# y of the later units: the state product as row tiles behind q kᵀ, a compact state, and a new written-out order

## The chip, the cores and the metric

The kernel runs on one core of a Trainium2 chip. The metric is the device time of one execution in microseconds. TensorE is PE in the profile (PEld its weight loads), VectorE is DVE, ScalarE is ACT, GpSimd is POOL, SyncE is SP.

## What is computed

A recurrent attention with a decaying state for 4 batches and 8 heads of width 48 over 768 positions, and behind it a two-layer network with a squared relu:

```python
for t in range(S):
    cur = np.einsum('bhd,bhe->bhde', u[None] * kt, vt)
    y[:, :, t] = np.einsum('bhd,bhde->bhe', rt, state + cur)
    state = w[None, :, :, None] * state + np.einsum('bhd,bhe->bhde', kt, vt)
...
h = x @ w_in
r = np.maximum(h, 0.0)
g = r * r
return (g @ w_out)
```

x is y of all heads side by side, 3072 rows of 384; w_in is 384 x 2048 and w_out 2048 x 384.

## The kernel before

**Units.** The sequence is cut into 6 chunks of 128 positions; a unit is one chunk of one batch, so there are 24, and unit i is chunk i // 4 of batch i % 4. Heads are handled in four pairs p; within a pair, head o = 0 lies on partitions 0 to 63 and head o = 1 on 64 to 127 (48 rows used, 16 zero).

**The order.** A string, SCHEDULE, lists every step as a word, `name:arguments@banks`. The words are run one after the other, each engine takes its own instructions in that order, and nothing reorders them. The numbers behind `@` are the PSUM banks (of 8) that the step's results take. `3*fill@4` is three times the step fill.

**The steps of a unit i.** `load:i:kt|rt|vt:queue` fetches k, r or v (192 KB) on the SP or POOL queue. `scale:i:0` multiplies r by powers of w and `scale:i:1` multiplies k by inverse powers (L287, DVE); the two tables of powers, wpos and wneg, are made once by `power:0` and `power:1` (L240, ACT) from the product of `spread_log` (L236). The scaled r and k are turned: for units 0 to 5 by `turn:i:x` on PE (L310) and `evict_rk:i:x` on ACT (L314), for later ones by `turn_dma:i` (L301, a transposing DMA of the SP queue). `rk` (L319, DVE) multiplies both for the diagonal term. `at:i` (L327) is q kᵀ: 8 matmuls that use 64 rows each, alternating between the two row halves, into two banks; `ats:i` does units i and i+1. `mask:i:o` (L339, DVE) takes out the upper triangle. `sums:i` (L347, L352) makes the diagonal sums and the unit's part of the state; it needs `uwb`, which POOL makes in `u_columns` (L251, L254) from `cols`, which DVE copies in `copy_columns` (L248). POOL also makes the decay over a whole chunk (`end_columns`, L257 and L259) and issues the four pieces of w_in (`win:q:0`, L273) and of w_out (`wout:q:0`, L278).

**y.** `y_mm:i` is 8 matmuls of the masked product with v (L390, 48 columns) and, from chunk 1 on, 4 of the turned r with the state (L396, 128 rows, 96 columns), whose bf16 copy `stb` holds the two heads of a pair as a block diagonal; `state_cast` (L381) writes it in two copies of 64 partitions. All twelve go into one bank. `diag_v` (L361) and `evict_y` (L405) finish y on DVE. `state_add` (L369, L371) and `state_decay` (L375) keep the state on DVE. y is turned by `x_turn` and `evict_x` (L420, L424) for units 0 to 5, and by `x_dma` (L414, SP queue) for later ones.

**The network.** `mm1:i:m:s` (L434) makes part of h for m units at once (m = 1 for units 0 to 7, m = 2 from 8 on); s counts the parts, 4 for m = 1 and 8 for m = 2, and for m = 1 part s needs piece s of w_in. `relu` (L442, ACT) and `square:...:a` (L451 on ACT where a is 1, L453 on DVE where it is 0) follow. `mm2:i:q` (L460) sums a quarter of the second product; `evict_o` (L467) and `store` (L494) bring it out. Unit 23 ends with `mm2_half` (L475), `evict_half` and `store_half` in two pieces.

`fill` (L232) is a matmul on constants whose result is not used: it fills waiting time of PE.

Of the kernel before, what the change touches and what calls it, by code (L numbers as in the profile page):

```python
# [9 lines left out]
BF16 = mybir.dt.bfloat16  # L10
# [12 lines left out]
fill@4 mask:1:1 turn:0:1@0 turn:2:0@1 scale:2:1 evict_rk:0:1 fill@4 fill@6 y_mm:1@2 diag_v:1 fill@6 win:3:0
evict_rk:2:0 2*fill@6 fill@0 rk:0 turn:2:1@3 fill@0 evict_y:1 load:3:vt:POOL evict_rk:2:1 at:0@4,5 2*fill@1 mask:0:0
fill@1 fill@2 cast_v:0 wout:0:0 at:2@6,0 load:6:rt:SP mask:0:1 cast_v:2 fill@3 fill@4 load:4:rt:POOL x_turn:1@1 fill@4
rk:2 sums:0@2 evict_x:1 fill@5 y_mm:0@3 diag_v:0 mm1:1:1:0@4 mask:2:0 wout:1:0 sums:2@5 evict_y:0 2*fill@1 2*fill@6
mask:2:1 x_turn:0@1 load:4:kt:POOL mm1:1:1:1@6 evict_x:0 diag_v:2 fill@0 scale:3:1 y_mm:2@3 relu:1:1:1 2*fill@1
mm1:0:1:0@0 evict_y:2 state_add:1 x_turn:2@1 turn:3:1@6 evict_x:2 mm1:0:1:1@3 evict_rk:3:1 mm1:2:1:0@7 scale:3:0
square:1:1:1:0 mm1:1:1:2@1 wout:2:0 relu:2:1:0 load:6:kt:SP state_add:2 relu:0:1:0 load:4:vt:POOL turn:3:0@6
mm1:0:1:2@7 evict_rk:3:0 mm1:2:1:2@0 relu:0:1:1 rk:3 wout:3:0 square:0:1:0:1 at:3@5,6 relu:1:1:0 load:5:vt:POOL  # L30
mm1:2:1:1@3 mask:3:0 relu:0:1:2 mm1:1:1:3@4 state_add:0 cast_v:3 square:2:1:0:1 mm1:2:1:3@5 square:0:1:1:0
square:1:1:0:1 sums:3@7 mask:3:1 mm1:0:1:3@2 relu:1:1:3 diag_v:3 relu:2:1:1 mm2:2:0@6 scale:4:0 relu:0:1:3 y_mm:3@4
mm2:0:0@3 relu:2:1:3 evict_y:3 relu:1:1:2 turn:4:0@2 x_turn:3@5 square:2:1:1:1 mm2:1:0@4 scale:4:1 evict_x:3
square:2:1:3:0 mm2:0:1 evict_rk:4:0 square:0:1:3:0 square:0:1:2:1 mm2:2:1 state_cast:0 square:1:1:3:0 turn:4:1@1
mm2:1:1 scale:5:1 evict_rk:4:1 mm1:3:1:2@5 square:1:1:2:0 relu:2:1:2 state_add:3 cast_v:4 mm1:3:1:1@2 load:9:kt:SP
mm2:0:2 scale:5:0 relu:3:1:1 load:7:kt:SP turn:5:1@1 state_cast:1 at:4@0,7 mm2:1:2 evict_rk:5:1 mask:4:1 load:8:kt:SP
square:2:1:2:1 turn:5:0@2 mask:4:0 mm1:3:1:0@1 evict_rk:5:0 load:7:rt:SP rk:4 y_mm:4@7 scale:6:0 relu:3:1:0 mm2:2:2
scale:6:1 relu:3:1:2 rk:5 at:5@0,2 cast_v:5 turn_dma:6 sums:4@1 state_cast:3 mm2:0:3 diag_v:4 square:3:1:0:1
mm1:3:1:3@5 mask:5:1 load:8:rt:SP square:3:1:1:1 evict_y:4 load:6:vt:SP mm2:1:3 relu:3:1:3 mask:5:0 sums:5@2
square:3:1:2:1 x_turn:4@7 mm2:2:3 load:9:rt:SP diag_v:5 evict_x:4 scale:7:1 evict_o:0 y_mm:5@5 scale:7:0 mm1:4:1:1@0  # L40
load:7:vt:SP state_add:4 mm1:4:1:0@7 evict_y:5 turn_dma:7 mm2:3:0@3 relu:4:1:0 scale:8:1 evict_o:1 at:6@1,5
square:4:1:0:0 evict_o:2 x_turn:5@7 load:10:kt:SP mm2:3:1 mask:6:0 evict_x:5 mm1:4:1:2@4 load:9:vt:SP scale:9:1 rk:6
mm2:3:2 relu:4:1:2 square:3:1:3:0 mm1:5:1:0@6 cast_v:6 scale:8:0 state_cast:2 sums:6@7 mask:6:1 turn_dma:8 mm2:3:3
square:4:1:2:1 diag_v:6 y_mm:6@1 relu:5:1:0 mm2:4:0@4 relu:4:1:1 evict_y:6 mm1:5:1:1@5 state_add:5 square:4:1:1:1
x_dma:6 rk:7 at:7@6,1 relu:5:1:1 scale:9:0 mm2:4:1 cast_v:7 mask:7:1 turn_dma:9 mm1:5:1:2@0 square:5:1:0:0 sums:7@2
mm1:5:1:3@5 mask:7:0 load:11:rt:SP state_add:6 mm1:4:1:3@1 load:10:rt:SP relu:5:1:3 y_mm:7@6 diag_v:7 load:8:vt:SP
relu:4:1:3 mm2:4:2 state_add:7 square:4:1:3:1 mm1:6:1:0@7 evict_y:7 mm2:4:3 x_dma:7 relu:6:1:0 relu:5:1:2
ats:8@5,1,2,6 square:6:1:0:0 square:5:1:1:1 load:11:vt:SP mm2:5:0@7 mask:8:0 square:5:1:3:1 load:11:kt:SP mm2:5:1
state_decay:5 evict_o:3 mask:8:1 load:12:kt:SP state_cast:5 mm2:6:0@0 state_decay:7 store:3:POOL mask:9:1 mm1:6:1:1@5
state_cast:7 store:1:POOL rk:8 mm1:6:1:3@3 cast_v:9 store:2:POOL rk:9 square:5:1:2:1 scale:10:1 store:0:POOL  # L50
mm1:6:1:2@1 scale:10:0 relu:6:1:1 sums:9@6 mask:9:0 relu:6:1:3 turn_dma:10 mm2:5:2 relu:6:1:2 diag_v:9 y_mm:9@5
cast_v:8 state_decay:4 mm1:7:1:0@3 evict_y:9 square:6:1:1:1 load:12:rt:SP sums:8@2 scale:11:0 state_cast:4 x_dma:9
mm2:6:1 diag_v:8 relu:7:1:0 y_mm:8@1 scale:11:1 mm1:7:1:1@5 state_add:8 turn_dma:11 mm1:7:1:3@3 evict_y:8 relu:7:1:1
square:7:1:0:0 mm1:7:1:2@2 relu:7:1:3 x_dma:8 state_add:9 mm2:5:3 square:6:1:2:1 cast_v:11 square:7:1:1:0 mm2:7:0@1
load:10:vt:SP relu:7:1:2 rk:10 load:13:rt:SP mm2:7:1 state_decay:9 square:7:1:2:0 load:13:kt:SP state_cast:9 mm2:6:2
square:6:1:3:0 square:7:1:3:1 mm2:7:2 load:13:vt:SP rk:11 evict_o:4 mm2:6:3 scale:12:0 evict_o:5 load:14:kt:SP
scale:12:1 ats:10@5,3,6,2 mm1:8:2:0@4 mask:10:1 turn_dma:12 mm1:8:2:4@7 mask:11:1 relu:8:2:0 mask:11:0 mm1:8:2:2@3
cast_v:10 load:14:rt:SP mask:10:0 sums:11@2 mm1:8:2:3@4 diag_v:11 mm1:8:2:1@6 scale:13:0 relu:8:2:3 state_decay:6
sums:10@5 relu:8:2:4 scale:13:1 y_mm:11@4 state_cast:6 mm2:7:3 turn_dma:13 evict_y:11 relu:8:2:2 mm1:8:2:7@7
square:8:2:0:0 relu:8:2:1 diag_v:10 y_mm:10@4 x_dma:11 square:8:2:3:1 mm1:8:2:6@3 square:8:2:1:0 square:8:2:4:1  # L60
mm1:8:2:5@6 evict_y:10 relu:8:2:6 load:12:vt:SP square:8:2:2:0 mm2:9:0@4 x_dma:10 relu:8:2:5 state_add:11 mm2:9:1
square:8:2:5:1 state_add:10 mm2:8:0@3 cast_v:13 load:15:kt:SP evict_o:6 state_decay:10 load:15:rt:SP mm2:8:1
relu:8:2:7 scale:14:1 load:16:kt:SP store:6:POOL evict_o:7 mm2:8:2 state_decay:8 rk:13 state_cast:8 store:4:POOL
square:8:2:7:0 ats:12@6,2,5,0 store:5:POOL scale:14:0 mm2:9:2 mask:13:1 turn_dma:14 sums:13@7 mm1:10:2:0@1
# [52 lines left out]
def kernel(  # L117
# [427 lines left out]
```

## Time and profile before

| | us |
|---|---|
| three runs: median (lowest to highest) | 174.15 (173.06 to 174.81) |
| the profiled execution | 172.5 |
| its span, first to last instruction | 170.4 |
| PE busy in the span | 163.4 |
| DVE busy | 137.0 |
| ACT busy | 120.9 |

The granted TensorE clock is 1.000 over the span. In the views below, times are microseconds from the span's start, and a row of the chain or the timeline gives a start, a length, the engine and line, and how many instructions were merged. A matmul's row includes its way through the array, so the pace of a group is read from the start of one group to the start of the next.

### The profile page before, as it was taken

What the parts mean: (1) busy time and instruction counts of PE and PEld (TensorE: products, weight loads), DVE (VectorE), ACT (ScalarE), POOL (GpSimd) and SP (SyncE); (2) the same over time, 40 slices, a digit from 0 to 9 for tenths busy, and PEclk for the clock granted to TensorE, in tenths of its full rate; (3) what the DMA queues carried; (4) which work ended last, traced back from release to release, by engine and by line L of the source; (5) the groups of instructions that cost most, each with busy time, mean ns of one, the idle gap of its engine ahead of it and who ended that gap; (6) DMA issues with size and microseconds to landing.
All of it is one profiled execution on the core that took longest, in us unless ns stands there. A gap on an engine that the chain in (4) does not pass through costs nothing.

```text
span 170.4 us, 4781 instructions
## 1 busy us (share of the span) xinstructions
PE 163.4 (96%) x1917; PEld 129.9 (76%) x1917; DVE 137.0 (80%) x297; ACT 120.9 (71%) x253; POOL 30.5 (18%) x62
## 2 busy tenths in 40 slices
PE   3899999999999999999999999999999999999993
PEld 2467998778778786795796895896898776999662
DVE  5359969969998999799988979988999898664800
ACT  3355489997685988579499499599359985295830
POOL 7989540000000500001100001203000030030010
PEclk9999999999999999999999999999999999999999
DMA  6999999989999999998999994998989994150014
GB/s 115 188 220 211 221 248 244 227 155 129 187 159 187 209 237 133 192 207 131 250 203 116 200 217 81 251 192 176 252 100 212 197 159 139 27 162 0 4 63 167
DMA packets 94784, 28.83 MB, mean 169 GB/s; under 512 B 90665, under 2 KB 92714, under 8 KB 94762
## 3 DMA queue, kind: packets, MB, share of 16 engines
q1 hardware_dynamic: 90512, 19.08, 73.9%
q0 software_dynamic: 4224, 9.44, 21.4%
q8 instruction: 15, 0.25, 0.6%
q14 instruction: 7, 0.06, 0.2%
q10 hardware_dynamic: 26, 0.00, 0.0%
HBM read 20.45 MB, written 4.72 MB: 148 GB/s over the span
## 4 chain that ended last, share of the span: by engine, by line
PE 84%; DVE 6%; DMA 5%; issue 1%; ACT 1%; ACTq 1%; DVEq 0%
PE bank L434 35%; PE bank L460 31%; PE bank L327 4%; DMA xT<-yb 3%; PE bank L390 3%; DMA rkT<-rkw 2%; PE bank L352 2%; PE bank L232 2%; PE bank L396 2%; PE bank L310 2%; PE bank L475 2%; DVE am L339 1%; DVE rkw L287 1%; PE bank L347 1%; DVE g L453 1%
## 5 line engine op out<-in xcount | busy, mean ns | idle before, releaser
L442 ACT ACTIVATE gr<-bank 128x512 f32<-128x512 f32 x96 | 53.1, 603 | 27.3 <-PE bank L434 25.9
L434 PE MATMUL bank<-xT,w_in_q 128*128 128x128 bf16 (+1 forms) x768 | 70.8, 246 | 0.6 <-DMA xT<-yb 0.4
L460 PE MATMUL bank<-w_out_q,g 128*128 128x384 bf16 x368 | 68.1, 327 | 0.1
L434 PEld LDWEIGHTS <-w_in_q 128*128 128x128 bf16 x768 | 64.2, 113 | 3.4 <-DMA xT<-yb 0.5
L460 PEld LDWEIGHTS <-g 128*128 128x128 bf16 x368 | 33.7, 98 | 19.2 <-DVE g L453 0.6
L453 DVE TENSOR_TENSOR g<-gr 128x512 bf16<-128x512 f32 x49 | 32.4, 686 | 6.9 <-ACT gr L442 6.8
L494 POOL DMA_DIRECT2D out_dram<-osb x21 | 11.3, 543 | 129.4 <-ACT osb L467 118.7
L339 DVE TENSOR_TENSOR am<-bank,smask 128x512 bf16<-128x512 f32 x48 | 31.4, 685 | 2.9 <-PE bank L327 2.8
L451 ACT ACTIVATE g<-gr 128x512 bf16<-128x512 f32 x47 | 29.1, 638 | 0.6
L287 DVE TENSOR_TENSOR rkw<-ldk,wneg 128x384 bf16<-128x384 f32 x24 | 13.2, 553 | 4.8 <-ACT wneg L240 3.6
L381 ACT CAST stb<-st 64x192 bf16<-64x192 f32 x40 | 13.9, 348 | 2.6 <-DVE st L375 2.3
L361 DVE TENSOR_TENSOR dv<-vb,bank 128x384 f32<-128x384 bf16 x24 | 13.0, 550 | 2.4 <-PE bank L352 1.5
L405 DVE TENSOR_TENSOR yb<-bank,dv 128x384 bf16<-128x384 f32 x24 | 13.3, 555 | 1.3 <-PE bank L396 0.3
L287 DVE TENSOR_TENSOR rkw<-ldr,wpos 128x384 bf16<-128x384 f32 x24 | 13.1, 553 | 1.0 <-DMA ldr<-in_r_dram 0.8
L319 DVE TENSOR_TENSOR rk<-rkT 128x512 bf16<-128x512 bf16 x24 | 10.0, 420 | 3.8 <-ACT rkT L314 2.0
L467 ACT COPY osb<-bank 128x384 f32<-128x384 f32 x23 | 10.5, 483 | 2.7 <-PE bank L460 2.7
L291 ACT CAST vb<-ldv 128x384 bf16<-128x384 f32 x24 | 12.1, 512 | 0.4 <-DMA ldv<-in_v_dram 0.3
L371 DVE TENSOR_TENSOR st<-bank,st 64x192 f32<-64x192 f32 x32 | 11.2, 351 | 1.2 <-PE bank L352 0.9
L232 PE MATMUL bank<-warm 128*128 128x256 bf16 x39 | 9.2, 334 | 2.0 <-DVE warm L183 1.5
L314 ACT COPY rkT<-bank 128x512 bf16<-128x512 bf16 x12 | 6.9, 595 | 3.7 <-PE bank L310 3.6
L390 PEld LDWEIGHTS <-am 128*128 128x128 bf16 x192 | 7.9, 96 | 2.0 <-issue 0.7
L327 PEld LDWEIGHTS <-rkT 64*128 64x128 bf16 x192 | 5.5, 96 | 4.2 <-issue 3.9
(58 smaller groups left out, 112.2 us busy)
## 6 DMA issues: line engine op xcount, KB each, us to landing
ldk<-in_k_dram SPq DMA_DIRECT2D x22, 192.0 KB, 4.6
out_dram<-osb POOLq DMA_DIRECT2D x21, 192.0 KB, 3.3
ldr<-in_r_dram SPq DMA_DIRECT2D x20, 192.0 KB, 3.7
ldv<-in_v_dram SPq DMA_DIRECT2D x19, 192.0 KB, 4.3
w_in_q<-in_moe_w_in_dram POOLq DMA_DIRECT2D x4, 384.0 KB, 8.9
w_out_q<-in_moe_w_out_dram POOLq DMA_DIRECT2D x4, 384.0 KB, 10.7
ldv<-in_v_dram POOLq DMA_DIRECT2D x5, 192.0 KB, 9.0
ldr<-in_r_dram POOLq DMA_DIRECT2D x4, 192.0 KB, 8.2
```

The lines of the kernel that those rows point to most:

```text
L232: nc.tensor.matmul(out=banks[given.pop(0)][:, :n], lhsT=warm[:, :128], rhs=warm[:, :n], start=True, stop=True)
L287: nc.vector.tensor_tensor(t["rkw"][:, x, :, :, :D], pair(src), pair(wx), ALU.mult)
L339: nc.vector.tensor_tensor(am, t["at"][o], smask.unsqueeze(1).to_broadcast([C, HP, C]), ALU.mult)
L361: nc.vector.tensor_tensor(t["dv"], t["vb"], t["d"].unsqueeze(2).to_broadcast([C, H, D]), ALU.mult)
L381: nc.scalar.copy(stb[b][sl, :, o * D : (o + 1) * D], st32[b][sl])
L390: nc.tensor.matmul(out=y[:, 2 * p + o, :], lhsT=t[f"am{o}"][:, p, :], rhs=t["vb"][:, 2 * p + o, :], start=(o == 0 and p == 0), stop=c == 0 ...
L405: nc.vector.tensor_tensor(t["yb"], t["y"], t["dv"].rearrange("p h d -> p (h d)"), ALU.add)
L434: nc.tensor.matmul(out=t["h", s][:, a], lhsT=turned, rhs=chunks[c]["xT"][:, n, b : b + m, :], start=(n == 0), stop=(n == NK - 1),)
L442: nc.scalar.activation(t["gr", s], t["h", s], AF.Relu)
L451: nc.scalar.activation(g, x, AF.Square)
L453: nc.vector.tensor_tensor(g, x, x, ALU.mult)
L460: nc.tensor.matmul(out=t["o"], lhsT=chunks[units[i][0]]["g"][:, f, units[i][1], :], rhs=w_out_q[f // 4][:, f % 4, :], start=(f == 0), stop ...
```

## The change

From unit 8 on, `ats:i` issues 16 more matmuls behind the 16 of q kᵀ: the turned r times the state, for each head by itself, 64 rows and 48 columns each, alternating between the row halves. The state's bf16 copy for them, `stc`, is 128 x 192 with no block diagonal, and `state_cast` writes it in one copy (for the states that units 8 and later read; units 4 to 7 go on with `stb` and `y_mm`). A new step `ys:i` adds the masked product with v for both units. The y of a pair takes two banks, one for each row half, both units side by side in each, from `ats` until it is evicted; `evict_y` has two instructions of 128 x 4 x 48 in place of one of 128 x 384.

SCHEDULE is written anew from its first line to its last. It has the same loads, stores, casts, turns and matmul steps apart from `y_mm` and `ys`, 38 fills instead of 39, and 8 squares more on ACT and 8 fewer on DVE. Its first lines and the code of the change (line numbers of what follows shift with it):

```diff
-load:1:kt:SP load:1:rt:POOL fill@7 load:0:rt:SP 2*fill@7 load:1:vt:POOL fill@7 load:0:kt:SP 3*fill@7 load:2:kt:SP
...
+load:1:kt:SP load:1:rt:POOL fill@6 load:0:rt:SP 2*fill@6 load:1:vt:POOL load:0:kt:SP load:2:kt:SP constants
...
+    Y_FROM = 8
...
+    stc = [const.tile([128, HP, D], BF16, name=f"stc_{b}") for b in range(B)]
...
+    def halves(i):
+        return [bank("y", i - i % 2, o).rearrange("p (u x) -> p u x", u=2)[:, i % 2, : dm // 2].rearrange("p (a d) -> p a d", a=HP) for o in range(2)]
+
     def ats(i):
         at(i)
         at(i + 1)
+        for j in (i, i + 1):
+            y = halves(j)
+            for p in range(HP):
+                for o in range(2):
+                    sl = slice(o * 64, o * 64 + 64)
+                    nc.tensor.matmul(
+                        out=y[o][:, p, :], lhsT=tiles[j]["rkT"][sl, 0, p, :], rhs=stc[units[j][1]][sl, p, :],
+                        start=(j == i and p == 0), stop=False, skip_group_check=True,
+                    )
...
     def state_cast(i):
         b = units[i][1]
-        for o in range(2):
+        if i >= Y_FROM - B:
+            nc.scalar.copy(stc[b], st32[b])
+        for o in range(2 if i < Y_FROM - B else 0):
             sl = slice(o * 64, o * 64 + 64)
             nc.scalar.copy(stb[b][sl, :, o * D : (o + 1) * D], st32[b][sl])
+
+    def ys(i):
+        for j in (i, i + 1):
+            t = tiles[j]
+            y = halves(j)
+            for p in range(HP):
+                for o in range(2):
+                    nc.tensor.matmul(
+                        out=y[o][:, p, :], lhsT=t[f"am{o}"][:, p, :], rhs=t["vb"][:, 2 * p + o, :],
+                        start=False, stop=j > i and p == HP - 1, skip_group_check=True,
+                    )
...
     def evict_y(i):
         t = tiles[i]
         t["yb"] = buffer("yb", [C, dm], BF16)
+        if i >= Y_FROM:
+            out_y = t["yb"].rearrange("c (a o d) -> c o a d", o=2, d=D)
+            dv = t["dv"].rearrange("c (a o) d -> c o a d", o=2)
+            for o, y in enumerate(halves(i)):
+                nc.vector.tensor_tensor(out_y[:, o], y, dv[:, o], ALU.add)
+            return
         nc.vector.tensor_tensor(t["yb"], t["y"], t["dv"].rearrange("p h d -> p (h d)"), ALU.add)
```

The order as built, at the places that the prediction speaks of. A name is a tile with its number: `rkw1` is the scaled r or k of unit 1, `ldk`, `ldr` loaded k and r, `bank5` is PSUM bank 5. The first place is DVE behind its setup, before the change:

```order
L287 TENSOR_TENSOR rkw1_116<-ldk1_102,wneg_93 128x8x48
L287 TENSOR_TENSOR rkw1_116<-ldr1_96,wpos_92 128x8x48
L248 COPY cols_94<-bank1_62 128x8
L287 TENSOR_TENSOR rkw0_115<-ldr0_95,wpos_92 128x8x48
L319 TENSOR_TENSOR rk_233<-rkT_211 128x512
L287 TENSOR_TENSOR rkw0_115<-ldk0_101,wneg_93 128x8x48
L287 TENSOR_TENSOR rkw2_117<-ldr2_97,wpos_92 128x8x48
```

DVE at the same place with the change, the lines two higher by the new code:

```order
L289 TENSOR_TENSOR rkw1_116<-ldk1_102,wneg_93 128x8x48
L289 TENSOR_TENSOR rkw1_116<-ldr1_96,wpos_92 128x8x48
L289 TENSOR_TENSOR rkw0_115<-ldk0_101,wneg_93 128x8x48
L289 TENSOR_TENSOR rkw0_115<-ldr0_95,wpos_92 128x8x48
L321 TENSOR_TENSOR rk_233<-rkT_215 128x512
L289 TENSOR_TENSOR rkw2_117<-ldk2_103,wneg_93 128x8x48
L250 COPY cols_94<-bank1_62 128x8
```

Both scalings of unit 0 have moved ahead of the first rk, and the copy of cols has moved from the third place to the seventh.

ACT at the first use of the log product (bank0) and the first turned tiles, before the change:

```order
L240 ACTIVATE wneg_93<-bank0_61,down_88 128x384
L240 ACTIVATE wpos_92<-bank0_61,up_86 128x384
L314 COPY rkT_211<-bank2_63 128x512
L314 COPY rkT_211<-bank3_64 128x512
L314 COPY rkT_228<-bank4_65 128x512
```

ACT with the change:

```order
L242 ACTIVATE wpos_92<-bank0_61,up_86 128x384
L242 ACTIVATE wneg_93<-bank0_61,down_88 128x384
L316 COPY rkT_215<-bank3_64 128x512
L316 COPY rkT_215<-bank2_63 128x512
L316 COPY rkT_227<-bank4_65 128x512
L316 COPY rkT_227<-bank5_66 128x512
```

The two tables have changed places; the half of unit 1 that is turned second (bank 3) is now copied first.

PE at the end of `ats:12`, whose banks were 6, 2, 5 and 0, before the change:

```order
L327 MATMUL bank5_66<-rkT_1599 128x128
L327 LDWEIGHTS rkT_1599
L327 MATMUL bank0_61<-rkT_1599 128x128
L460 LDWEIGHTS g_1611
L460 MATMUL bank4_65<-w_out_q2_155,g_1611 128x384
```

PE at the end of q kᵀ in `ats:12` with the change:

```order
L329 MATMUL bank7_68<-rkT_1605 128x128
L329 LDWEIGHTS rkT_1605
L329 MATMUL bank4_65<-rkT_1605 128x128
L345 LDWEIGHTS rkT_1547
L345 MATMUL bank5_66<-stc_0_149,rkT_1547 128x48
```

Sixteen products with the state, which go to banks 5 and 1 in turn, now stand between q kᵀ and the second product of the network, and they take two more banks.

More of the change, by code (lines that the diff above doesn't have):

```diff
@@ L23 @@
[L23 to L62, printed above, removed]
```

149 lines of the change are left out of this document (94 added, 55 removed).

## Prediction

> **What bounds the kernel now.** I read the engine shares and slices of the page first, then the chain of waits, then the chain and the timelines of the first 22 us, where the two orders differ most.
>
> ```profile
> PE 163.4 (96%) x1917; PEld 129.9 (76%) x1917; DVE 137.0 (80%) x297; ACT 120.9 (71%) x253; POOL 30.5 (18%) x62
> PE   3899999999999999999999999999999999999993
> PEclk9999999999999999999999999999999999999999
> PE 84%; DVE 6%; DMA 5%; issue 1%; ACT 1%; ACTq 1%; DVEq 0%
> ```
>
> PE is busy in every slice but the first two and the last, and the chain is PE for 84%: the end is the time at which PE gets real work, plus all the work left then, plus waits. The chain in order of time gives each step's price:
>
> ```profile
> 7.54 0.61 PE bank L310 x4
> 8.15 0.21 PE bank L232
> 13.44 0.44 PE bank L232 x4
> 13.88 0.22 PE bank L310 x4
> 18.42 0.67 PE bank L434 x12
> 24.25 0.33 PE bank L327 x8
> 28.30 0.20 PE bank L390 x8
> 29.38 0.17 PE bank L420 x3
> 31.73 0.65 PE bank L460 x4
> 36.77 0.17 PE bank L396 x4
> 55.28 0.55 PE bank L327 x16
> 78.26 4.59 DMA xT<-yb
> 88.68 0.65 PE bank L434 x6
> 164.96 2.65 PE bank L475 x32
> ```
>
> An mm1 costs 0.67 (one unit) or 0.65 (two), an mm2 0.65, q kᵀ 0.33 alone and 0.55 for two units, y 0.20 + 0.17, a fill 0.11. Early matmuls run at half that pace: a fill takes 0.21 at 8.15 and 0.11 from 13.44. In the same way the PE timeline gives the sums (0.11 for L347, start to start, and 0.17 for L352), and three further places:
>
> ```profile
> 20.12 0.33 PE L420 MATMUL bank<-identb,yb 128*128 128x128 bf16 x3
> 61.69 0.25 PE L347 MATMUL bank<-uwb,rk 128*128 128x8 bf16 x4
> 61.80 0.33 PE L352 MATMUL bank<-vb,rkw 128*128 128x96 bf16 x4
> 82.90 4.12 PE L434 MATMUL bank<-xT,w_in_q 128*128 128x256 bf16 x36 [0.35 <-DMA xT<-yb]
> ```
>
> 20.12 is `x_turn:2`, from which on PE of the kernel before never lacks work for long. The words behind it cost 144.3 at these prices (34.3 of them up to `ats:8`), and PE ends at 164.96 + 2.65 = 167.6, so all its waits after 20.3 come to 3.0. There is little to gain behind the start.
>
> **The start.** ACT, DVE and POOL in the first 22 us, and how long the transfers took that hang on them:
>
> ```profile
> 6.31 0.58 ACT L240 ACTIVATE wneg<-bank,down 128x384 f32<-128x384 f32 x1 [1.73 <-PE bank L236]
> 6.79 0.58 ACT L240 ACTIVATE wpos<-bank,up 128x384 f32<-128x384 f32 x1
> 8.19 1.71 ACT L314 COPY rkT<-bank 128x512 bf16<-128x512 bf16 x3 [0.82 <-PE bank L310]
> 6.92 0.56 DVE L287 TENSOR_TENSOR rkw<-ldk,wneg 128x384 bf16<-128x384 f32 x1 [3.59 <-ACT wneg L240]
> 7.87 0.16 DVE L248 COPY cols<-bank 128x8 f32<-128x8 f32 x1
> 9.44 0.43 DVE L319 TENSOR_TENSOR rk<-rkT 128x512 bf16<-128x512 bf16 x1 [0.95 <-ACT rkT L314]
> 14.58 1.29 DVE L339 TENSOR_TENSOR am<-bank,smask 128x512 bf16<-128x512 f32 x2
> 19.46 0.55 DVE L405 TENSOR_TENSOR yb<-bank,dv 128x384 bf16<-128x384 f32 x1
> 19.93 0.71 DVE L369 TENSOR_TENSOR st<-bank,wend_c 64x192 f32<-64x192 f32 x2
> 9.24 0.69 POOL L254 CAST uwb<-cols 64x4 bf16<-64x4 f32 x2
> 9.85 0.77 POOL L273 DMA_DIRECT2D w_in_q<-in_moe_w_in_dram  x1
> 11.88 1.84 POOL L259 TENSOR_TENSOR wend_c<-wend_c 128x4 f32<-128x4 f32 x6
> 13.74 0.76 POOL L273 DMA_DIRECT2D w_in_q<-in_moe_w_in_dram  x1
> DMA to landing us min/median/max: 7.2/8.9/10.2
> DMA to landing us min/median/max: 2.3/3.7/5.6
> ```
>
> The last two rows are of w_in and of the turned y (xT). DVE's first scaling, of k of unit 1, needs wneg, which ACT now makes second: it starts 0.48 later (6.79 less 6.31), at 7.40. The second scaling follows 0.47 later (a 128x384 operation is followed by the next after 0.47, 19.46 to 19.93), so the second turn starts where this scaling has run 0.6, at 8.5 to 8.6. ACT now copies the half that is turned second first, which it can from about 9.2 (0.65 behind its turn, as 8.19 is behind 7.54), and the two copies take 1.71 x 2/3 = 1.14: rk of unit 1 starts at about 10.5, not 9.44. From there to the end of `evict_y:2` DVE has in its order 8 operations of 128x384 (0.47 each, 3.8), 6 masks (1.29 for two, 3.9), 3 rk (0.43, 1.3), 3 pairs of state sums (0.71, 2.1) and the copy of cols (0.2), 11.3 with tails, some 0.8 less where one's tail lies under the next one's start: 20.9 to 21.0. On PE the words up to `x_turn:2` leave it free at 21.5 (y of unit 1 is evicted at 16.2 by the same count, and between it and `x_turn:2` stand five mm1, 3.35, and 1.95 of fills, sums, turns and y). So `x_turn:2` stands at 21.5 where it stood at 20.12: **+1.4**, between +0.4 (no tail or handover lost) and +2.4 (another microsecond for loads of units 0 and 2, now needed sooner, or for matmuls still at half pace).
>
> By then the new order has issued five mm1 and not three: **-1.34**. But 13 of its 38 fills come after this point, against none before: 13 x 0.108 = **+1.40**. In part they cover waits that the kernel before had: from the end of `x_turn:2` (20.12 + 0.17) to `ats:8` it used 55.28 - 20.29 = 35.0 for words worth 34.3, so I give back **-0.4**, between 0 and -0.7.
>
> **w_in.** POOL's order of work is the same, but `u_columns` waits for the copy of cols, now behind rk and a scaling: 10.5 + 0.4 + 0.5 = 11.4 where it was 7.87. POOL is then free for the third piece of w_in at about 12.3 (9.85 before) and, with a load and the 2.1 of `end_columns` ahead, for the fourth at about 16.1 (13.74). The first mm1 of part 3 stands 1.4 of PE work behind `x_turn:2` (x_turn, a fill, an mm1, two turns): at 22.9, where before it stood at 25.1. The nearest rows give a landing at 16.1 + 7.2 = 23.3 to 16.1 + 10.2 = 26.3, waits of 0.4 to 3.4; but the pieces before landed behind a queue of loads that now has had longer to drain, which favours the short end. I take **+0.4**; ends 0 and +3.4.
>
> **The state as row tiles.** Per unit 4 matmuls at 0.17 together go, 8 come. L347 with 8 columns takes 0.11 for four and L390 with 48 columns 0.20 for eight: neither goes below 0.025 each. So 8 x 0.025 = 0.20 against 0.17, for 16 units: **+0.5**. Ends: q kᵀ has the same row halves at 128 columns for 0.55 / 16 = 0.034 each, +1.7; if 48 columns cost that in proportion, 8 x 0.013 = 0.10, -1.1. I stay with the floor, which two rows of nearly this size show.
>
> q kᵀ of one unit takes 0.33 and of two 0.55, so a visit to row tiles costs a fixed 2 x 0.33 - 0.55 = 0.11. The Trainium skill (TensorEngine Tiling, Key Properties) says that a change of tiling mode drains TensorE, and the trace agrees. By that rule the eight state groups, were they to stand apart, would add 8 x 0.11 = 0.9; directly behind q kᵀ they add none, and the sum stays.
>
> **DVE and ACT.** These rows price the other edits:
>
> ```profile
> L405 DVE TENSOR_TENSOR yb<-bank,dv 128x384 bf16<-128x384 f32 x24 | 13.3, 555 | 1.3 <-PE bank L396 0.3 <-ACT gr L442 0.3 <-issue 0.2
> L381 ACT CAST stb<-st 64x192 bf16<-64x192 f32 x40 | 13.9, 348 | 2.6 <-DVE st L375 2.3
> L375 DVE TENSOR_TENSOR st<-st,wend_c 128x192 f32<-128x192 f32 x16 | 5.6, 352 | 0.1
> ```
>
> Eviction of y becomes two of about 0.35: 16 x (0.70 - 0.555) = 2.3 more on DVE; eight squares fewer take 8 x 0.69 off it. ACT gets eight squares and loses 16 casts of 0.348. Both stay below PE's 163.4, which hides them: 0. If DVE ran late, PE would stand at `ys`: `ats` now takes six of eight banks, and in the shortest case (units 18 and 19) 3.1 of PE words and 0.4 of state tiles cover four masks and an rk, 2.6 + 0.4. SP and POOL queues carry as many transfers as before; a late store delays nobody but the last, and the last words on PE and their stores are the same: 0.
>
> **Turned y.** At 82.90 PE waited for a transfer that took 4.59 and had 4.1 of PE words in front of it. The new order gives that unit (10) 4.9, but units 15 and 18 only 3.6 and 3.3 (`x_dma:15 mm2:13:2 mm2:13:3 ... mm2:12:1 ... ats:16 ... mm2:12:2 ... mm1:14:2:2`) and 9 and 13 4.2. At the median of 3.7 that is 0.1 + 0.4, less the 0.35 gone: **+0.1**. Ends: -0.5 (fast transfers) and +2.7 (all four at 4.6).
>
> **Sum.** 1.4 - 1.34 + 1.40 - 0.4 + 0.4 + 0.5 + 0.1 = +2.1, on the profiled execution's 172.5 (span 170.4) 174.6. The median of the runs, 174.15, lies 1.65 above that execution, and I put the same difference on it: 176.2.
>
> **The rivals.**
> 1. *The fourth piece of w_in decides.* It lands at the median 8.9 behind 16.1, 25.0, PE stands 2.1 at 22.9, 1.7 more than in my sum: 177.9, up to 179.2 at 10.2. For it: all four pieces took 7.2 to 10.2. Against it: the emptier queue.
> 2. *Not slower: the waits for transfers go.* The median lies 1.65 above the profiled execution; if that and 0.85 of the 2.2 of waits that the sum leaves behind the start are transfers that come late, and the new distances and fills absorb them, the sum is 176.2 - 1.65 - 0.85 = 173.7; with a start only 0.4 later, 172.7. It decides if mm1 waits for xT by less than 0.1 in all. For it: DMA holds the chain for 5%. Against it: the four shorter distances above.
> 3. *The half pace lasts.* The new order has 3 fills and not 7 ahead of the log product, and PE idles more until 12. If matmuls kept the pace of 8.15 until the five early mm1 are through, these would cost 5 x 0.67 more, half of that if it ends midway: +1.7, 177.9. The Trainium skill (TensorE: Matmul & The Clock Gate, What's actually happening) says that the clock halves after an idle window of about 3.4 us and rises after a busy one. The profile's clock row (PEclk) shows no such step; the two paces of the fill do.
> 4. *The tiles do not run side by side,* or each pair waits for its six banks: +1.2 (the upper end above), 177.4.
>
> **How the numbers follow.** Chances: my forecast, 174.7 to 177.3, 0.47; rival 1, 0.16; rival 2, 0.24; rival 3, 0.06; rival 4, 0.07. The range reaches to the lower end of rival 2 and the upper of rival 1, 172.7 to 179.2, and leaves out less than 2 in 10. One per cent, about what a measurement of this kernel can tell from no change, is 1.74: faster is below 172.4, slower above 175.9. Slower: 0.27 of my forecast's part, and all of rivals 1, 3 and most of 4: 0.53. Faster: the low tail of rival 2, 0.13. The rest, 0.34, is within.
>
> **What would show it.** Right: the first scaling on DVE at about 7.4, the first rk near 10.5, the copy of cols near 11.4, `x_turn:2` (third L453 group) near 21.5, the state tiles about 0.40 for sixteen, and no wait above 1 us on PE behind 25. Wrong: an mm1 that waits for w_in; half-pace groups past 15; sums of waits for xT above 1; or a PE that ends near 167 because the start was made up.

## The result and the profile after

The changed kernel takes 174.45 us (median of 20 runs, 173.57 to 177.43), the kernel before 173.24 (20 runs, 171.85 to 177.06). The ratio of the two is 1.0113, with a 95% interval of 1.0086 to 1.014: slower by 1.96 us, 1.5 to 2.4. This ratio is taken over the fast runs alone, without those at a lowered clock, while the medians, over all 20 runs each, differ by 1.21. The forecast was +2.1 us and slower. The profiled execution of the changed kernel took 174.41 us, its span is 172.6, and both are 1.9 to 2.2 above the one before. The forecast's 176.2 lies 1.75 above the measured median. Of this 0.91 is not in the change: the forecast was built on the median of the three runs shown, 174.15, which 20 runs put at 173.24.

From the page of the changed kernel come its engine shares, PE's row of slices and the chain by engine:

```profile
PE 162.6 (94%) x1980; PEld 129.3 (75%) x1980; DVE 132.3 (77%) x305; ACT 119.3 (69%) x245; POOL 30.1 (17%) x62
PE   1797999999999999999999999999999999899993
PE 80%; DVE 9%; DMA 3%; issue 2%; ACT 2%; ACTq 1%; POOL 0%; DVEq 0%
```

PE does 0.8 us less work than before and ends later: the rest is waiting, and DVE has gone from 6% of the chain to 9%. The timelines of DVE, POOL and PE in the first 22 us show the start:

```profile
7.43 0.56 DVE L289 TENSOR_TENSOR rkw<-ldk,wneg 128x384 bf16<-128x384 f32 x1 [4.11 <-ACT wneg L242]
10.44 0.43 DVE L321 TENSOR_TENSOR rk<-rkT 128x512 bf16<-128x512 bf16 x1 [1.04 <-ACT rkT L316]
11.25 0.16 DVE L250 COPY cols<-bank 128x8 f32<-128x8 f32 x1
15.83 0.76 POOL L275 DMA_DIRECT2D w_in_q<-in_moe_w_in_dram  x1
12.52 0.27 PE L234 MATMUL bank<-warm 128*128 128x256 bf16 x1
12.65 0.40 PE L312 MATMUL bank<-identb,rkw 128*128 128x128 bf16 x4
21.82 0.34 PE L453 MATMUL bank<-identb,yb 128*128 128x128 bf16 x3
```

Every step of the start stands within 0.35 us of its forecast (7.4, 10.5, 11.4, 16.1, 21.5). The fill at 12.52 takes 0.13 to the next group: full pace from there, so the half pace did not last. The chain in order of time gives the prices of q kᵀ (L329), of the state row tiles (L345), of the masked product for two units (L405) and the last group of PE:

```profile
59.65 0.55 PE bank L329 x16
60.21 0.20 PE bank L345 x16
65.05 0.40 PE bank L405 x16
167.06 2.65 PE bank L508 x32
```

The tiles of L345 start in pairs, by the starts of the single instructions in the trace: the two of a pair, one in each row half, are 0.003 to 0.004 us apart, and the next pair follows 0.025 us after the one before it. q kᵀ has the same pairs, 0.056 apart at its 128 columns.

PE ends at 169.71, 2.1 after the 167.6 of before. `ats:8` starts at 59.65 where it stood at 55.28 (59.59 and 55.21 in the timeline, which counts from the first instruction's start and not from the end of the group ahead). The list of PE's waits has no row of 1 us behind the setup; four of its rows:

```profile
PE bank L312 <- DVE rkw L289: 0.8, 1, 0.8
PE bank L467 <- DVE dv L375: 0.5, 1, 0.5
PE bank L329 <- DMA rkT<-rkw: 0.3, 1, 0.3
PE bank L467 <- DVE am L353: 0.2, 1, 0.2
```

These sum to little, and yet PE needs 37.7 us from the end of `x_turn:2` (21.82 + 0.17) to `ats:8` for words that cost 35.7 at the prices of the prediction (20 mm1, 22 mm2, 13 fills and the small ones). Before, it was 35.0 for 34.3. So 2.0 us stand there beyond the words in place of 0.7, in gaps of 0.1 to 0.5, and most of them are not in the list. In both kernels 0.55 of this is not waiting: behind each of the five q kᵀ of this stretch the next group takes 0.10 to 0.12 more than elsewhere. In the chain of the kernel before, an mm2 behind q kᵀ takes 0.76, where an mm2 takes 0.65:

```profile
34.59 0.33 PE bank L327 x8
34.92 0.76 PE bank L460 x4
```

What is left is 1.45 of waits in the changed kernel and 0.15 in the kernel before, whose chain has no other engine than PE from 19.95 us to `ats:8`. The chain of the changed kernel leaves PE in this stretch, and the longest piece, 3.9 us, is on DVE:

```profile
39.27 0.20 PE bank L366 x4
39.56 0.55 DVE dv L375
40.78 1.03 DVE rkw L289 x2
41.84 0.56 DVE yb L438
42.73 0.61 DVE am L353
43.39 2.20 PE bank L467 x36
```

It leads from the sums of unit 4 to the mask that frees the bank of an mm1, and two scalings of k for units 8 and 9 stand in the middle of it. PE has other words for most of these 3.9 us, and gaps of some 0.7 in all.

### The profile page after: what moved, and what is told of

It reads as the page before. It is cut to its first block, busy times and chain, and to the rows that moved or that the text cites. A ratio compares the mean times of both kernels' runs of the same rounds, so it can differ in the third digit from the quotient of the medians.

```text
span 172.6 us, 4914 instructions
## 1 busy us (share of the span) xinstructions
PE 162.6 (94%) x1980; PEld 129.3 (75%) x1980; DVE 132.3 (77%) x305; ACT 119.3 (69%) x245; POOL 30.1 (17%) x62
## 3 DMA queue, kind: packets, MB, share of 16 engines
q1 hardware_dynamic: 90512, 19.08, 67.4%
q0 software_dynamic: 4224, 9.44, 21.5%
## 4 chain that ended last, share of the span: by engine, by line
PE 80%; DVE 9%; DMA 3%; issue 2%; ACT 2%; ACTq 1%; POOL 0%; DVEq 0%
PE bank L467 34%; PE bank L493 32%; DMA rkT<-rkw 3%; PE bank L329 3%; DVE am L353 2%; PE bank L366 2%; PE bank L405 2%; DVE dv L375 2%; PE bank L508 2%; PE bank L312 1%; DVE yb L438 1%; DVE rkw L289 1%; DVE st L383 1%; PE bank L361 1%; PE bank L238 1%
## 5 line engine op out<-in xcount | busy, mean ns | idle before, releaser
L475 ACT ACTIVATE gr<-bank 128x512 f32<-128x512 f32 x96 | 55.5, 602 | 22.7 <-PE bank L467 22.0
L486 DVE TENSOR_TENSOR g<-gr 128x512 bf16<-128x512 f32 x41 | 27.5, 688 | 11.6 <-ACT gr L475 11.5
L484 ACT ACTIVATE g<-gr 128x512 bf16<-128x512 f32 x55 | 33.9, 632 | 0.5
L436 DVE TENSOR_TENSOR yb<-bank,dv 128x192 bf16<-128x192 f32 x32 | 9.7, 351 | 2.4 <-PE bank L405 2.1
L234 PE MATMUL bank<-warm 128*128 128x256 bf16 x38 | 9.7, 307 | 1.5 <-DVE warm L183 1.5
L329 PE MATMUL bank<-rkT 64*128 64x128 bf16 x192 | 8.7, 222 | 1.1 <-ACT rkT L316 0.7
L329 PEld LDWEIGHTS <-rkT 64*128 64x128 bf16 x192 | 5.7, 96 | 5.3 <-issue 2.8
L457 ACT COPY xT<-bank 128x384 bf16<-128x384 bf16 x6 | 2.9, 479 | 6.8 <-PE bank L453 6.8
## 6 DMA issues: line engine op xcount, KB each, us to landing
w_out_q<-in_moe_w_out_dram POOLq DMA_DIRECT2D x4, 384.0 KB, 10.5
```

Of the source, the lines that this page charges most:

```text
L329: nc.tensor.matmul(out=t["at"][o][:, p, :], lhsT=t["rkT"][sl, 1, p, :], rhs=t["rkT"][sl, 0, p, :], start=True, stop=True,)
L475: nc.scalar.activation(t["gr", s], t["h", s], AF.Relu)
L484: nc.scalar.activation(g, x, AF.Square)
L486: nc.vector.tensor_tensor(g, x, x, ALU.mult)
```

## The experiments

Three stretches are compared throughout: to the third `x_turn` (unit 2), from there to `ats:8`, and from there to PE's end. These are starts in each profiled execution, in us, with the ratio of the times to the kernel before:

| kernel | `x_turn:2` | `ats:8` | PE's end | ratio |
|---|---|---|---|---|
| before | 20.12 | 55.21 | 167.59 | 1 |
| changed | 21.82 | 59.59 | 169.70 | 1.0113 [1.0086, 1.014] |
| e1_start | 21.41 | 59.87 | 170.72 | 1.0114 [1.0062, 1.0166] |
| e2_nofill | 21.95 | 59.54 | 169.96 | 1.0109 [1.0066, 1.0151] |
| e3_both | 21.62 | 59.36 | 169.33 | 1.0114 [1.0072, 1.0157] |
| e8_k6 | 21.34 | 58.92 | 169.00 | 1.0083 [1.0047, 1.0119] |
| e12_k_on_pool | 21.31 | 58.51 | 168.36 | 1.0078 [1.0041, 1.0114] |

Each row is one execution, so small differences say little. The changed kernel, e4_old_y, e5_apart, e6_two_casts and e10_pool_cast have the same words up to `ats:8`, and put `x_turn:2` at 21.75 to 21.89 and `ats:8` at 59.54 to 59.90: up to 0.4 is scatter.

### The start and the fills

e1_start gives the start of the new order the old one's sequence at three places; everything behind is the changed kernel.

```diff
-power:0 ... power:1 ... evict_rk:1:0 ... evict_rk:1:1
+power:1 ... power:0 ... evict_rk:1:1 ... evict_rk:1:0
-scale:1:0 ... rk:1 ... copy_columns u_columns
+scale:1:0 copy_columns u_columns ... rk:1
```

> The changed kernel with its start put back in three points: wneg is made before wpos, the half of unit 1 that is turned first is copied first, and the copy of cols stands third on DVE again (u_columns right behind it). Theory A (the late start and the fills make the time, PE is the bound from the third L453 group on): the first scaling starts near 6.95, the first rk near 9.45, x_turn:2 near 20.8 instead of 21.8, and the end comes 1.0 us earlier: ratio to the kernel before about 1.0055. Rival B (what is gained at the start is lost again before unit 8, because DVE, ACT or transfers set the pace from 22 to 60 us): x_turn:2 comes earlier, ats:8 stays at 59.6, ratio about 1.011.

Measured: 1.0114. `x_turn:2` came 0.4 earlier, `ats:8` 0.3 later, which is within the scatter: the gain was lost on the way. DVE's timeline names two of the places:

```profile
31.41 0.56 DVE L290 TENSOR_TENSOR rkw<-ldk,wneg 128x384 bf16<-128x384 f32 x1 [0.76 <-DMA ldk<-in_k_dram]
35.94 0.56 DVE L290 TENSOR_TENSOR rkw<-ldk,wneg 128x384 bf16<-128x384 f32 x1 [1.25 <-DMA ldk<-in_k_dram]
```

These are the scalings of k of units 5 and 6. In the changed kernel k of unit 5 is there in time, and k of unit 6 is waited for:

```profile
36.05 0.56 DVE L289 TENSOR_TENSOR rkw<-ldk,wneg 128x384 bf16<-128x384 f32 x1 [1.67 <-DMA ldk<-in_k_dram]
```

e2_nofill takes out the 13 fills behind `x_turn:2`, and e3_both does that and the edit of e1_start.

```diff
-x_turn:2@5 fill ... 12 more fills up to ats:8
+x_turn:2@5 ...
```

> The changed kernel without the 13 fills behind x_turn:2; all else as it is. Theory A: a fill costs its 0.108 us whether or not anything is awaited, and PE is the bound there: 13 x 0.108 = 1.4 us less, ats:8 near 58.2, ratio about 1.003. Rival B: the fills stand where PE would wait anyway, the time goes into waits: ats:8 stays within 0.4 us of 59.6, ratio about 1.010.

> The changed kernel with both edits: its start put back in the three points and the 13 fills behind x_turn:2 taken out. Each alone left ats:8 at 59.5 to 59.9. Rival B (loads and DVE set the pace from 22 to 60 us: k of unit 6 lands at 36.0 and its scaling stands ahead of rk, masks and evictions on DVE): ats:8 within 0.5 us of 59.6, ratio to the kernel before about 1.010. Theory A in a weaker form (either of the two was enough to hide the other's gain): ats:8 1 to 2 us earlier, ratio 1.000 to 1.005.

Measured: `ats:8` moved by 0.05 in e2_nofill and by 0.23 in e3_both, and both ratios are that of the changed kernel. Of the 1.40 us of fills taken out, 1.2 came back as waits in e2_nofill and 1.4 in e3_both: the fills covered waits and cost next to nothing. So neither the later start nor the fills set the time of `ats:8`, alone or together. Something that runs beside PE does.

### The loads of k

SP's queue shows how long it stands at a single load; this is k of unit 9 in the changed kernel, a start and the time until the queue goes on:

```profile
19.01 12.98 SPq L268 DMA_DIRECT2D ldk<-in_k_dram  x1
```

And over all loads of k the time from issue to landing, in the changed kernel:

```profile
DMA to landing us min/median/max: 3.1/4.9/17.8
```

In e3_both the same row has a maximum of 23.3, for a piece of 192 KB. The kernel before has 22.7, so such slow loads are not new. But its DVE waits for no load between 12 and 85 us: it comes to the scaling of k of unit 6 at 36.97. In the changed kernel DVE is there at 34.4, before the load has landed, and the words behind it wait as well.

The page's rows on the queues tell how they differ (packets, MB, share of time; q1 is SP's, q0 POOL's):

```profile
q1 hardware_dynamic: 90512, 19.08, 67.4%
q0 software_dynamic: 4224, 9.44, 21.5%
```

19.08 MB in 90512 packets is 0.21 KB each, 9.44 MB in 4224 is 2.2 KB each. The same rows of the DMA view for 24 to 32 us alone, when POOL's queue brings the weights and DMA is busy at 90% or more in every slice:

```profile
q0 software_dynamic: 630, 1.79, 96.2%
q1 hardware_dynamic: 628, 0.12, 11.6%
```

The two queues move the same number of packets, and POOL's moves fifteen times the bytes. The Trainium skill (DMA: Bandwidth & Descriptors, Queues, rings and completion order) says that each DMA engine takes turns between its queues packet by packet; the trace agrees, with 630 packets against 628, and 637 against 660 in the same 8 us of the kernel before.

e8_k6 is e3_both with k of unit 6 ahead of r of unit 6 in SP's queue; e12_k_on_pool is e3_both with k of units 5 and 6 issued by POOL. Of each queue only its own words are shown here; other words stand between them.

```diff
 e8_k6
-load:6:rt:SP load:6:kt:SP
+load:6:kt:SP load:6:rt:SP
 e12_k_on_pool
-load:5:kt:SP load:6:rt:SP load:6:kt:SP
+load:6:rt:SP
-load:4:kt:POOL wout:2:0 load:4:vt:POOL wout:3:0
+load:4:kt:POOL load:5:kt:POOL wout:2:0 load:4:vt:POOL load:6:kt:POOL wout:3:0
```

> As the kernel with both edits (start put back, no late fills), and on the SP queue k of unit 6 is fetched ahead of r of unit 6. Theory B1 (the wait of DVE for k of unit 6, 1.3 to 1.7 us at 36, is what holds the stretch): that scaling starts near 34.5, ats:8 comes 0.7 us or more earlier than with both edits alone, ratio about 1.004. Rival B2 (the wait only fills a time in which DVE waits for PE, or the next load is late instead): ats:8 within 0.3 us of both edits alone.

> e3_both (early start, no fills) with the loads of k of units 5 and 6 issued by POOL, behind k of unit 4 and v of unit 4, instead of by SyncE, whose queue took over 20 us for them; DVE waited 0.57 and 1.55 us for them in e3_both. Theory B (what holds the stretch from 22 to 60 us is these transfers on SyncE's queue): the two waits go, q k^T of unit 8 begins at 57.5 to 58.5 us instead of 59.36, ratio to before 1.000 to 1.006. Rival G (all transfers together hold it: the same megabytes must land by then): other loads are late instead, q k^T of unit 8 stays within 0.5 us of 59.36, ratio 1.008 to 1.014.

Measured: in e8_k6 the wait for k of unit 5 is gone and the one for unit 6 stays:

```profile
35.48 0.56 DVE L289 TENSOR_TENSOR rkw<-ldk,wneg 128x384 bf16<-128x384 f32 x1 [1.79 <-DMA ldk<-in_k_dram]
```

`ats:8` stands 0.44 earlier than in e3_both, about the scatter. In e12_k_on_pool both waits are gone, `ats:8` stands 0.85 earlier than in e3_both (0.3 of it already at `x_turn:2`) and PE's end 0.97 earlier. The ratios 1.0083 and 1.0078 lie 0.3% under that of the changed kernel, though the intervals overlap. The numbers fall at the edge between the two theories: the two loads were part of what holds this stretch, worth 0.5 to 0.9 us, and not the whole. From the end of `x_turn:2` e12_k_on_pool still needs 37.0 us for 34.3 of words, 2.8 beyond them where the kernel before had 0.7. The remaining gaps stand behind DVE (a turn that waits 0.32 for a scaling at 32.0, some 0.8 around the masks and y at 41 to 42.5). The chain says the same: without the fills and the two late loads it runs on DVE from 25.66 to 32.02 and from 38.52 to 42.42, some 10 of the 37 us. What order of DVE's words would shorten this was not tried.

### The state tiles, the casts and the evictions

e5_apart takes the 16 state tiles out of `ats` and puts them ahead of the masked products in `ys`; the y banks are still taken in `ats`.

```diff
     def ats(i):
         at(i)
         at(i + 1)
-        for j in (i, i + 1): ... nc.tensor.matmul(out=y[o][:, p, :], lhsT=...["rkT"][sl, 0, p, :], rhs=stc...)
...
     def ys(i):
+        for j in (i, i + 1): ... nc.tensor.matmul(out=y[o][:, p, :], lhsT=...["rkT"][sl, 0, p, :], rhs=stc...)
```

> The changed kernel with the 16 row tiles of each pair moved from behind q k^T to the front of the masked product with v, so that they stand apart from q k^T; all else as it is. Theory A (a visit to row tiles costs a fixed 0.11 us, as 2 x 0.33 - 0.55 shows, 0.10 of which the changed kernel's rows show between the last tile and the next full matmul): 8 x 0.11 = 0.9 us slower than the changed kernel, ratio about 1.0165. Rival D (no fixed cost, the gain of the place behind q k^T is nil): ratio about 1.011.

Measured: 1.0234 [1.0196, 1.0272], 2.1 us over the changed kernel; PE's ends in the two profiled executions differ by 2.1 too. PE's timeline in one pair, the tiles now L399 and between mm1 (L470) and the masked product (L408):

```profile
76.26 1.47 PE L470 MATMUL bank<-xT,w_in_q 128*128 128x256 bf16 x12
77.67 0.37 PE L399 MATMUL bank<-stc,rkT 64*128 64x48 bf16 x16
77.97 0.58 PE L408 MATMUL bank<-vb,am 128*128 128x48 bf16 x16
78.39 0.81 PE L496 MATMUL bank<-w_out_q,g 128*128 128x384 bf16 x4
```

The tiles take 0.30 from their start to the next group, and mm1 ahead of them 1.41 instead of 1.30. With the 0.20 that the chain gives for sixteen, a visit to row tiles costs 0.1 on the way in and 0.1 on the way out. Directly behind q kᵀ one such visit is shared. The Trainium skill (TensorEngine Tiling, Key Properties) says that a change of mode drains TensorE; the trace agrees, with 0.2 a visit, twice the 0.11 that the prediction had taken from q kᵀ of one and of two units. Eight visits are 1.6 of the 2.1; a wait of 0.70 for xT ahead of 149.9 us, 0.25 longer than the one on dv there in the changed kernel, is part of the rest. The 0.11 was only one half: the other is the 0.10 to 0.12 that the group behind q kᵀ takes more, as the chain of the kernel before already had it.

e4_old_y keeps the new order and goes back to the old y: full-height state product with the block diagonal `stb`, two casts, one bank a unit, one eviction.

```diff
-    Y_FROM = 8
+    Y_FROM = 100
...
-                        out=y[o][:, p, :], lhsT=tiles[j]["rkT"][sl, 0, p, :], rhs=stc[units[j][1]][sl, p, :],
...
+                    lhsT=t["rkT"][:, 0, p, :], rhs=stb[units[j][1]][:, p, :],
```

> The changed kernel's order with the former way of making y: no row tiles behind q k^T, the state product with 128 rows and 96 columns behind the masked product, from the block-diagonal state, one bank for each unit, two casts and one eviction as before. Theory A: a pair's q k^T and state products took 0.46 + 0.30 us in the changed kernel and 0.55 + 2 x 0.17 before, so this undoes a gain of 0.13 for each of 8 pairs: 1.0 us slower than the changed kernel, ratio about 1.017. Rival C (the two more banks held, the second eviction or the earlier need of the state cost more than the tiles save): not slower than the changed kernel, ratio 1.011 or less.

Measured: 1.0337 [1.0279, 1.0396], 3.9 us over the changed kernel. PE's own rows explain 8 x (0.34 - 0.20) = 1.1 of it. The rest stands as waits on ACT, above all one in front of mm2:

```profile
142.05 2.76 PE L493 MATMUL bank<-w_out_q,g 128*128 128x384 bf16 x16 [1.89 <-ACT osb L500]
```

e6_two_casts asks whether the casts do it. It is the changed kernel with `stc` written in two copies of 64 partitions.

```diff
-            nc.scalar.copy(stc[b], st32[b])
+            for o in range(2):
+                sl = slice(o * 64, o * 64 + 64)
+                nc.scalar.copy(stc[b][sl], st32[b][sl])
```

> The changed kernel with the compact state written in two copies of 64 partitions instead of one of 128; y and its order as in the changed kernel. Theory E (ACT is close enough to PE's pace that 16 more copies of 0.35 us reach PE through late evictions of banks, which is what made the old form of y cost 3.9 us where PE's own rows explain 1.0): 1.5 to 3 us slower than the changed kernel, ratio 1.020 or more. Rival F (casts are hidden, as the prediction had it): ratio about 1.011.

Measured: 1.0244 [1.0193, 1.0296], 2.3 us over the changed kernel; the profiled span is 3.0 longer. The group of the casts and the same wait in front of mm2:

```profile
L397 ACT CAST stc<-st 64x192 bf16<-64x192 f32 x32 | 11.1, 348 | 0.3
141.72 2.76 PE L496 MATMUL bank<-w_out_q,g 128*128 128x384 bf16 x16 [1.25 <-ACT osb L503]
```

A copy of 64 partitions takes 348 ns, one of 128 partitions takes 360 in the changed kernel: half the partitions save nothing, so two copies are 16 x 0.336 = 5.4 us more on ACT, an engine that is busy 69% of the span, and 2.3 of these come out at the end. This is most of what e4_old_y lost beside PE's rows.

e10_pool_cast goes the other way and gives the casts to POOL.

```diff
-            nc.scalar.copy(stc[b], st32[b])
+            nc.gpsimd.tensor_copy(stc[b], st32[b])
```

> The changed kernel with the compact state cast by POOL instead of ACT (16 casts of 128x192; ACT loses 5.7 us of work, POOL gains 16 instructions whose length no run has shown). e6_two_casts doubled these casts on ACT, and the time rose by about 2.3 us. Theory E (ACT's load is what cost it: PE waits for the relus and squares that stand behind the casts): the casts' cost goes with them, 0.5 to 2 us faster than the changed kernel, ratio to before 1.000 to 1.008. Rival F (the delay between the sum of the state and the row tiles cost it, 0.36 us a pair): POOL's cast is longer than ACT's, so the time stays or rises, ratio to before 1.011 to 1.03, with PE waiting for stc ahead of the row tiles.

Measured: 1.009 [1.0056, 1.0123], between the two theories, and the profiled PE ends 0.45 later than in the changed kernel. POOL's casts take 540 ns as a mean, and nothing on PE waits for them:

```profile
L395 POOL CAST stc<-st 128x192 bf16<-128x192 f32 x16 | 8.6, 540 | 36.6 <-DVE st L390 36.6
```

So 5.4 us more on ACT cost 2.3 us, and 5.7 less bring about 0.4, which the intervals do not tell from nothing. ACT is not the bound of the changed kernel, but it is close to being one. Whether e6_two_casts lost by ACT's load alone or also by the later `stc` isn't settled.

### The old order up to unit 8, the new one behind it

If the stretch ahead of unit 8 is what loses, the old order up to `ats:8` and the new one with the new y behind it should beat both. Three seams were made. In e7_splice the words that the new order has done by `ats:8` and the old one has not stand in a row ahead of it. In e9_splice2 q kᵀ comes first and those words behind it. In it the second product of units 3 and 4 is evicted after its banks were taken again, so this part of the output is not computed, and its q kᵀ does not wait for the two evictions; the instructions are the same. In e11_splice3 these evictions stand ahead again, and the scalings and turns of units 10 and 11 earlier.

```diff
 e7_splice: old order ... relu:5:1:2
+... square:5:1:3:1 ... square:5:1:2:1 ... square:5:1:1:1 rk:9 mm2:5:0@0 evict_o:3 ... mm2:5:1 evict_o:4 mm1:6:1:1@2 ... rk:8
 ats:8@4,3,1,7,6,5 ... new order
 e9_splice2: old order ... relu:5:1:2
+rk:8 ... rk:9 state_cast:4 ats:8@4,3,1,7,6,5 mm1:6:1:1@2 square:5:1:3:0 square:5:1:2:1 square:5:1:1:0 ... mm2:5:0@0 ... mm2:5:1 ...
 ... new order
```

> The order of the kernel before up to unit 8 (all its words ahead of ats:8, its start and its fills with it), then the words that the new order has done by then, then the new order with the new form of y. Theory: the start and the stretch to unit 8 cost the changed kernel 59.6 - 55.3 = 4.3 us, of which 1.3 is work done sooner; behind ats:8 it needed 110.1 where the kernel before needed 112.3. So here ats:8 comes near 57.2 (three more words of PE ahead of it, 1.97) and PE ends about 109.4 later, near 166.6 instead of 167.6: ratio about 0.994. Rival (what the new order needs behind ats:8 hangs on the transfers that its own start brought earlier or later): no faster than the kernel before, ratio 1.000 or more.

> As e7_splice, but at the seam the q k^T of units 8 and 9 comes before the work that the old order has not done by then: one piece of mm1 and two of mm2 of chunk 5 and 6 now stand behind q k^T, and two of the three squares that they wait for are on DVE instead of ACT. In e7_splice PE waited 0.52 + 1.16 us at that seam for ACT. Theory S (the later start of the new order, and not the new y, is what is lost; e7_splice hid it by a seam that was badly made): the seam's 1.7 us go, q k^T of unit 8 begins at 54.5 to 55.5 us, the span is near 171, the ratio to before 0.997 to 1.0. Theory T (behind unit 8 the new order is held by transfers, so what is won ahead is waited away): the seam's wait goes, but rkT by DMA is waited for longer, above all near 138 us, where e7_splice already waited 1.30; the ratio stays at 1.004 to 1.010.

> A third seam between the old order up to unit 8 and the new order behind it. In e9_splice2 the two evictions that must free banks for q k^T stood too late, so its outputs were partly overwritten; here they stand ahead of it. The load of k of unit 11, the four scalings of units 10 and 11 and their two turns by DMA stand earlier, since e9_splice2 waited 0.38 + 0.53 us for those turned tiles and 0.59 us for a turned xT behind them. Theory S (only the late start of the new order is lost): those waits go, and nothing takes their place; about 1.5 us less than e9_splice2, ratio to before 0.994 to 0.999. Theory T (behind unit 8 SyncE's queue and DVE pace the new order, whatever the start): the waits come back at another transfer within the next two pairs, ratio 1.001 to 1.008.

Measured: 1.0082 [1.0045, 1.0119], 1.0048 [1.001, 1.0087] and 1.0116 [1.0058, 1.0174]. None beats the kernel before. PE's timeline of e7_splice shows the seam itself, two mm2 that wait for squares and relus in a row on ACT:

```profile
55.32 0.81 PE L494 MATMUL bank<-w_out_q,g 128*128 128x384 bf16 x4 [0.52 <-ACT gr L476]
57.29 0.82 PE L494 MATMUL bank<-w_out_q,g 128*128 128x384 bf16 x4 [1.16 <-ACT g L485]
```

e9_splice2 starts `ats:8` at 56.05 with two mm2, 1.3 us, less done than the changed kernel at its 59.59: a lead of 2.2. PE ends at 169.74, and in this execution the lead is gone. By the ratios e9_splice2 is 1.1 us faster than the changed kernel, with intervals that just meet, so up to half of the lead may be left. What took most of it here:

```profile
57.13 0.38 PE L346 MATMUL bank<-stc,rkT 64*128 64x48 bf16 x16 [0.46 <-ACT stc L395]
69.18 0.40 PE L330 MATMUL bank<-rkT 64*128 64x128 bf16 x8 [0.38 <-DMA rkT<-rkw]
70.11 0.40 PE L330 MATMUL bank<-rkT 64*128 64x128 bf16 x8 [0.53 <-DMA rkT<-rkw]
73.36 2.79 PE L468 MATMUL bank<-xT,w_in_q 128*128 128x256 bf16 x24 [0.59 <-DMA xT<-yb]
```

1.5 us of it is transfers that did not come earlier when PE did. e11_splice3 was to get the turned tiles of units 10 and 11 ahead. One of them is waited for again, and the mm1 behind it starts when it did in e9_splice2, 73.32 against 73.36. DVE's timeline and PE's:

```profile
68.61 1.03 DVE L290 TENSOR_TENSOR rkw<-ldk,wneg 128x384 bf16<-128x384 f32 x2 [1.20 <-DMA ldk<-in_k_dram]
69.49 0.40 PE L330 MATMUL bank<-rkT 64*128 64x128 bf16 x8 [0.82 <-DMA rkT<-rkw]
73.32 2.78 PE L468 MATMUL bank<-xT,w_in_q 128*128 128x256 bf16 x24 [1.08 <-DVE am L354]
111.83 1.47 PE L468 MATMUL bank<-xT,w_in_q 128*128 128x256 bf16 x12 [0.98 <-DMA xT<-yb]
```

DVE waits 1.20 for another load of k, so that the masks behind it come when they did in e9_splice2 (71.90 against 71.87), and PE waits for a mask instead of xT. The theory that only the late start is lost gave 0.994 to 1.0 for these seams, and falls with them. That SP's queue and DVE pace the new order behind unit 8 agrees with all three; e11_splice3 is slower than that theory gave, and what adds the rest is open. Each seam brought waits of its own, so it is not shown that no seam could win.

## Why the prediction was right, and where it was wrong

The sign and the size were right, +2.1 against +1.96 [1.5, 2.4]. That the sum came out is in large part luck: two of its terms were wrong by 1.7 and 1.6 us in opposite directions. Point by point, against the profiled executions:

| step | forecast | measured | from |
|---|---|---|---|
| `x_turn:2` later | +1.4 | +1.7 | 21.82 - 20.12 |
| two more mm1 done by then | -1.34 | -1.3 | five mm1 ahead of 21.82; by `ats:8`, two mm2 more |
| 13 fills, and the waits that they cover | +1.40 - 0.4 | +2.7 | 37.7 - 35.0, `x_turn:2` to `ats:8` |
| fourth piece of w_in | +0.4 | 0 | no mm1 waits for w_in |
| state as row tiles | +0.5 | -1.1 | 8 x (0.20 - 2 x 0.17) |
| turned y and all else behind `ats:8` | +0.1 | +0.1 | what is left of the 2.1 |

*The start* was read rightly, each of its instructions from the row that releases it. Only the way from the first rk to `x_turn:2` took 0.3 longer.

*The fills and waits ahead of unit 8* are the first step that failed: "In part they cover waits that the kernel before had [...] so I give back -0.4". The fills cover waits wholly, as e2_nofill shows, but waits of the new order's own. Nor was the 0.7 that the forecast gave part of back made of waits: 0.55 of it is the way back from row tiles behind five q kᵀ, which both orders have. The forecast counted PE's words alone between `x_turn:2` and `ats:8` and took the waits of the old order as the new one's upper bound. e1_start, e3_both and e12_k_on_pool show a stretch that PE does not set: an earlier start and fewer fills leave `ats:8` where it was, and loads of k that come earlier move it by 0.85. Of the 2.7, words are 1.4 (the 13 fills) and waits 1.3; without the fills the waits are larger by about as much. The two loads of k are 0.5 to 0.9 us of it. For the rest the chain names DVE, whose words in this stretch no run reordered, so this cause stays open.

*The state tiles* are the second: "neither goes below 0.025 each [...] I stay with the floor, which two rows of nearly this size show". Both rows, L347 and L390, are full-height matmuls. Row tiles alternate between two halves of the array, and sixteen of them take 0.20, 0.0125 each. The floor itself holds, but for a pair: two tiles that start almost together cost the 0.025 of one full-height matmul. The right row was the one set aside, q kᵀ, which has the same row halves: 0.034 at 128 columns, in proportion 0.013 at 48, the lower end of -1.1. The Trainium skill (TensorE: Matmul & The Clock Gate, Wait — 56ns, not 53.3ns?) gives the same floor of about 25 ns from start to start; the trace has it between full-height matmuls and from pair to pair, and between the two tiles of a pair the measurement decides: 3 to 4 ns.

*The casts and squares at 0* came out in the sum, but not for the reason given, that PE's work hides them. e6_two_casts shows that the same 16 casts, put back into this order, are not hidden but cost 2.3. The single cast of the compact state and the order need each other, and the order spends the room on eight more squares on ACT.

*w_in and turned y* stood on ends far apart, and the short end of both was right: PE waited nowhere for w_in (in e4_old_y and e10_pool_cast, with the same start, it did for 0.2), and mm1's wait for xT of before is gone. All turned y by DMA landed within 4.5 us, at a median of 2.5 where it had been 3.7.

*The rivals.* Rival 1 (w_in) and rival 3 (half pace) are answered by the rows above: no wait, and full pace from 12.5. Rival 4 fails by the 0.20. Rival 2 (not slower) asked for waits behind the start that go. 0.35 for xT went, 0.45 for dv and 0.32 for a turned tile came.

## What to carry to other kernels

When an order is rewritten, add up PE's words for each stretch, and next to that the same for each queue and each other engine: the stretch takes at least the longest of them, and taking words off PE where another sets the pace only uncovers its waits. A floor for small matmuls belongs to the way in which they use the array; price row tiles by row tiles. A term that is given back as waiting has to be waiting: look first for what the neighbours of a group pay. Copies like these cost by their count and not by their partitions, so a layout that needs one copy instead of two is worth something as soon as the engine is near its limit, even if the profile calls it hidden.

## What the runs showed of the hardware

- Sixteen matmuls of 64 rows and 48 columns on alternating row halves take 0.20 us: the two of a pair start 0.003 to 0.004 apart, and a pair follows the other after 0.025, the pace of full-height matmuls of the same columns. A visit to row tiles from full-height matmuls costs 0.1 in and 0.1 out.
- A copy on ACT of 64 x 192 from f32 to bf16 takes 348 ns and of 128 x 192 360 ns; the latter takes 540 ns on POOL.
- While POOL's queue loaded weights in large packets and SP's queue k and r in small ones, each moved the same number of packets (630 and 628 from 24 to 32 us), with 1.79 MB against 0.12. A load of 192 KB on SP's queue took up to 23.3 us from issue to landing, and a single issue held SP's queue for 12.98 us. Loads of k issued by POOL landed after 10.0 us at the median in e12_k_on_pool, and DVE no longer waited for them.
